# Two transformer layers on one core: a second static order of 3098 steps, with other engine homes and other PSUM banks

## The chip, the cores and the metric

The kernel runs on one core of one Trainium2 chip. A core has a matrix engine (TensorE, PE in the profile, with its weight loads shown as PEld), a vector engine (VectorE, DVE), an activation engine (ScalarE, ACT), a general engine (GpSimd, POOL), a queue that issues transfers (SyncE, SP) and 16 DMA engines. Each engine works through its own list of instructions in order; engines meet only at semaphores. The metric is the device time of one execution in microseconds, as a median over runs; less is better.

## What is computed

The input `x` is 2048 rows of 512 numbers in bf16. Four blocks follow one another, A, B, A, B, with the same weights each time:

```python
def _A_ref(x, wqkv, wo):
    H = 32; Dh = D // H; W = 256
    q, k, v = ...                       # x @ wqkv, split into 32 heads of 16
    scores = jnp.einsum("bhqd,bhkd->bhqk", q, k) * (Dh ** -0.5)
    mask = (i - j >= 0) & (i - j < W)   # a sliding window of 256 keys
    p = _softmax(jnp.where(mask, scores, -1e9))
    return jnp.einsum("bhqk,bhkd->bhqd", p, v) ... @ wo

def _B_ref(x, w1, b1, w2, b2):
    return _gelu(x @ w1 + b1) @ w2 + b2     # 512 -> 1792 -> 512

x = x + _A_ref(_layernorm(x), A_wqkv, A_wo)
x = x + _B_ref(_layernorm(x), B_w1, B_b1, B_w2, B_b2)
x = x + _A_ref(_layernorm(x), A_wqkv, A_wo)
x = x + _B_ref(_layernorm(x), B_w1, B_b1, B_w2, B_b2)
```

## The kernel before

All weights and the whole of `x` stay in SBUF. The work of both layers is cut into 16 attention blocks of 256 rows (8 per layer; b0 to b15) and ten MLP jobs of 256 or 512 rows (m0 to m9). Because the window is 256 keys, block b of the second layer needs only a few blocks of the first, so attention of one part runs beside the MLP of another.

One attention block consists of these steps, each with a short name that the texts below use with the block's number:

- layer norm: statistics `bs`, `ba` on VectorE; for all but the first pair of rows the inverse root on GpSimd (`vp` adds epsilon, on GpSimd or VectorE; `pw` is the power -0.5, on GpSimd); `xn` applies it on VectorE; a DMA transpose on SyncE's queue (`tx`) or, for the first four and the last two row tiles, a transpose on TensorE (`tp`) with an eviction `te` on VectorE or ScalarE
- projections `q`, `k`, `v` on TensorE, evictions `qe` and `ve` on VectorE or ScalarE, `ke` on VectorE; `vs` is a shifted copy of V by DMA
- 10 visits (5 in the first block of a layer): scores `sc` (TensorE, into four PSUM banks, allocated as two pairs), two exponentials `ex` on ScalarE that each free one pair, and masks `mk`, multiplications in place on VectorE or GpSimd
- twice per block `pv` (TensorE, probabilities times V, into a pair of banks), its transpose `od` out of PSUM, `rc`, `nm` (VectorE or GpSimd) and `ot`; `od` frees the pair of banks for the next scores
- the output projection `op` and the residual `rs`, and the second layer norm

An MLP job has 14 groups of first matmuls with gelu on ScalarE (six go through VectorE's `gb` and a paired gelu `ga`, eight are direct, `ge`), then per row tile 14 second matmuls `y` and the sum `ya` on VectorE with `Xb`, which GpSimd prepares (`xb`). The last row tile, y31, is done in two halves of 256 columns.

At the start 18 matmuls on zeros (`warm`) keep TensorE busy; GpSimd writes constants (among them `ia`, a memset of V's column of ones in all ten V buffers, `Va[:, :, :, Dh:VW]`, and `pidx`), and VectorE makes `parmask` from `pidx` in two small steps, `i5` and `i6`, which the first `ke` needs.

What sets the order is not the code's loops. Every step is recorded in a list of 3098 nodes (`add` in `_Plan`), and three tables replay it: `_ORDER` is the global sequence, from which each engine's list is the subsequence of its own steps (so it sets SyncE's transfers too); `_ALT` lists the steps that take their second home (a mask on GpSimd, an eviction on ScalarE, and so on); `_BANKS` gives the PSUM bank of each allocation in turn. `_Sched` then derives the semaphore waits from what each step reads and writes.

## Time and profile before

| | |
|---|---|
| median of 3 runs | 441.85 us (441.66 to 443.46) |
| span of the profiled execution | 442.4 us (its only time on the page; 0.55 us over the median, inside the runs' range) |
| TensorE busy | 416.1 us, 94% of the span |
| ScalarE busy | 386.4 us, 87% |
| VectorE busy | 341.0 us, 77% |
| GpSimd busy | 212.7 us, 48% |
| mean granted TensorE clock | 0.996 |

A window row reads: the stretch in us from the span's start, its length, then for each engine the busy us and the number of instructions, then the granted clock of TensorE (1.00 is full), the share of the DMA engines and GB/s. A timeline row reads: start, length, engine, line, operation, what it writes from what it reads, the shapes, the count of merged instructions, and in brackets how long the engine sat idle before and what released it. A row of the chain of waits reads: start, length, engine and line, count.

### The profile page before, as it was taken

The numbers are of one execution on the slowest core, as the hardware profiler recorded it, in microseconds if no ns is written. First come the engines' busy times: TensorE is split into PE (matmuls) and PEld (weight loads), VectorE is DVE, ScalarE is ACT, GpSimd is POOL, SyncE is SP. The second block draws the span as 40 slices with busy tenths as digits, with TensorE's granted clock in tenths as the row PEclk, the third lists the DMA queues.
The fourth block names the chain that finished last, engine by engine and source line by source line (L and its number), as shares of the span: only waits on it lengthen the run. The fifth ranks groups of instructions, "written<-read, shape, count | busy, mean of one in ns | idle before, by whom it ended". The sixth has DMA issues, their size and how long they took to land.

```text
span 442.4 us, 16864 instructions
## 1 busy us (share of the span) xinstructions
PE 416.1 (94%) x7523; PEld 233.2 (53%) x7593; DVE 341.0 (77%) x638; ACT 386.4 (87%) x458; POOL 212.7 (48%) x236
## 2 busy tenths in 40 slices
PE   8997999988789997999999999999999999999997
PEld 4555657544444563554455455455555464444675
DVE  7997789788785599967698868877888576746762
ACT  4997999999889999889899989999897988999533
POOL 3566344363442674711575454634728165804411
PEclk9999999999899999999999999999999999999999
DMA  7686422004101012121031021100421014003002
GB/s 234 184 209 185 87 64 45 20 10 69 39 3 25 16 34 56 28 46 24 4 65 31 1 57 26 34 20 10 69 39 20 20 39 105 14 1 81 15 0 73
DMA packets 48116, 23.25 MB, mean 53 GB/s; under 512 B 33196, under 2 KB 48044, under 8 KB 48044
## 3 DMA queue, kind: packets, MB, share of 16 engines
q1 hardware_dynamic: 48044, 22.17, 22.2%
q8 instruction: 60, 0.98, 0.9%
q14 instruction: 12, 0.10, 0.1%
HBM read 8.00 MB, written 2.10 MB: 23 GB/s over the span
## 4 chain that ended last, share of the span: by engine, by line
PE 79%; ACT 11%; DVE 6%; issue 2%; DMA 1%; DVEq 0%
PE ps L653 59%; PE ps L754 9%; PE ps L804 9%; ACT E L761 9%; DVE OD L813 1%; PE ps L539 1%; DVE stat L599 1%; DVE X L849 1%; DMA xnTB<-xn 1%; ACT gT L879 1%; ACT L879 1%; DVE KT L687 1%; DVE E L782 0%; PE ps L639 0%; ACT QT L590 0%
## 5 line engine op out<-in xcount | busy, mean ns | idle before, releaser
L761 ACT ACTIVATE E<-ps 128x1024 bf16<-128x1024 f32 x300 | 284.2, 1033 | 28.7 <-PE ps L754 28.0
L782 POOL TENSOR_TENSOR E<-E,mask 128x512 bf16<-128x512 bf16 (+2 forms) x111 | 120.9, 1106 | 91.3 <-ACT E L761 91.0
L653 PE MATMUL ps<-W_sb,gT 128*128 128x512 bf16 (+1 forms) x434 | 112.2, 373 | 3.2 <-issue 2.2
L653 PE MATMUL ps<-xnTB,W_sb 128*128 128x512 bf16 (+1 forms) x541 | 107.8, 336 | 3.4 <-issue 1.8
L653 PEld LDWEIGHTS ps<-xnTB,W_sb 128*128 128x128 bf16 x560 | 52.0, 98 | 42.9 <-issue 4.1
L653 PE MATMUL ps<-xnTA,Wqkv_sb 128*128 128x256 bf16 x512 | 70.7, 273 | 0.9 <-ACT E L761 0.4
L782 DVE TENSOR_TENSOR E<-E,mask 128x512 bf16<-128x512 bf16 (+2 forms) x125 | 60.1, 500 | 13.3 <-ACT E L761 12.9
L754 PE MATMUL ps<-QT,KT 32*128 32x128 bf16 (+3 forms) x1920 | 60.3, 231 | 9.8 <-ACT E L761 5.6
L653 PEld LDWEIGHTS ps<-W_sb,gT 128*128 128x128 bf16 x462 | 41.2, 98 | 41.1 <-issue 3.6
L754 PEld LDWEIGHTS ps<-QT,KT 32*128 32x128 bf16 x1920 | 28.5, 92 | 59.1 <-ACT E L761 34.9
L653 PEld LDWEIGHTS ps<-xnTA,Wqkv_sb 128*128 128x128 bf16 x512 | 47.4, 98 | 20.2 <-issue 2.9
L813 DVE STREAM_TRANSPOSE OD<-ps 128x1024 f32<-128x1024 f32 x32 | 39.9, 1246 | 21.3 <-PE ps L804 20.7
L887 POOL TENSOR_TENSOR Xb<-X,b2all 128x512 f32<-128x512 bf16 x32 | 37.7, 1180 | 34.3 <-DVE X L894 33.9
L879 ACT ACTIVATE gT<-ps,b1T 128x512 bf16<-128x512 f32 (+1 forms) x80 | 42.6, 609 | 9.5 <-PE ps L653 9.4
L804 PE MATMUL ps<-E,Va 64*17 64x128 bf16 (+3 forms) x1920 | 44.3, 234 | 1.9 <-issue 0.8
L821 POOL TENSOR_TENSOR Nb<-OD,Rc 128x512 bf16<-128x512 f32 x25 | 26.4, 1058 | 38.7 <-DVE Rc L817 29.8
L804 PE MATMUL ps<-E,Vs 64*17 64x128 bf16 (+3 forms) x1920 | 44.9, 234 | 0.0
L599 DVE BATCH_NORM_STATS2 stat<-X 128x6 f32<-128x512 bf16 x64 | 42.9, 679 | 0.5
L804 PEld LDWEIGHTS ps<-E,Va 64*17 64x17 bf16 x1920 | 37.2, 85 | 11.6 <-issue 9.0
L871 DVE TENSOR_SCALAR gT<-ps,b1T 128x512 bf16<-128x512 f32 (+1 forms) x60 | 36.8, 632 | 6.6 <-PE ps L653 6.2
L687 DVE TENSOR_TENSOR KT<-ps,parmask 128x1024 bf16<-128x1024 f32 x32 | 38.7, 1211 | 3.6 <-PE ps L653 3.6
L804 PEld LDWEIGHTS ps<-E,Vs 64*17 64x17 bf16 x1920 | 38.0, 85 | 0.2
(55 smaller groups left out, 348.8 us busy)
## 6 DMA issues: line engine op xcount, KB each, us to landing
Vs<-Va SPq DMA_DIRECT2D x64, 68.0 KB, 2.0
W_sb<-in_B_w_dram SPq DMA_DIRECT2D x4, 512.0 KB, 4.8
out_dram<-X SPq DMA_DIRECT2D x15, 128.0 KB, 1.8
X<-in_A_x_dram SPq DMA_DIRECT2D x3, 512.0 KB
Wqkv_sb<-in_A_wqkv_dram SPq DMA_DIRECT2D x4, 256.0 KB, 4.5
W_sb<-in_B_w_dram SPq DMA_DIRECT2D x2, 384.0 KB, 7.1
W_sb<-in_B_w_dram SPq DMA_DIRECT2D x1, 768.0 KB, 5.0
Wqkv_sb<-in_A_wqkv_dram SPq DMA_DIRECT2D x1, 512.0 KB, 6.7
```

Source lines behind the costliest of these rows:

```text
L599: add("dve", lambda e, B, t=t, k6=k6: e.bn_stats(stat6[:, k6, :], X[:, t, :]), reads=["X%d" % t], writes=["st%d" % k6], key="bs%d" % (k + j))
L653: r = e.matmul(ps[:, B[g][0], cols], lhsT, rhs, start=st, stop=sp)
L687: add("dve", lambda e, B, g=g, i=i: e.tensor_tensor(out=KT[:, kb, 2 * i : 2 * i + 2].rearrange("p c m a q -> p a (c m) q"), in0=ps[:, B[g] ...
L754: x = e.matmul(ps[:, bk[r], o : o + n], KT[rows, kb, c, m].rearrange("p a q -> p (a q)"), QT[rows, c, q : q + n], start=True, stop=True)
L761: add("act", lambda e, B, g_=g_, gi=gi: e.activation(E[:, 2 * gi : 2 * gi + 2, e0 : e0 + 512], ps[:, B[g_][0] : B[g_][0] + 2, :], AF.Exp, ...
L782: fn = lambda e, B: e.tensor_tensor(out=Ew, in0=Ew, in1=Mw, op=ALU.mult)
L804: x = e.matmul(ps[32 * r : 32 * r + VW, B[g][par], c % 2 * 2 * P + lo : c % 2 * 2 * P + hi], V[rows, (2 * b + m // 2) % VR, c * HC + 2 * r ...
L813: add("dve", lambda e, B: e.transpose(OD[:, s].rearrange("p a c q -> p (a c q)"), ps[:, B[g][0] : B[g][0] + 2, :]), reads=["ps:" + g], wri ...
L821: return e.tensor_tensor(out=Nb[:, s, :].rearrange("p (k a d) -> p a k d", a=2, d=Dh), in0=sums[:, :, :, 0:Dh], in1=rc[:, :, :, None].to_b ...
L871: add("dve", lambda e, B, g=g, fc=fc: e.tensor_scalar(out=gT[:, fc, c0 : c0 + M], in0=ps[:, B[g][0], 0:M], scalar1=b1T[:, fc : fc + 1], sc ...
L879: add("act", lambda e, B, g=g, fc=fc: e.activation(gT[:, fc, c0 : c0 + M], ps[:, B[g][0], 0:M], AF.Gelu_apprx_tanh, bias=b1T[:, fc : fc + ...
L887: add("pool", lambda e, B, t=t, xs=xs: e.tensor_tensor(out=Xb[:, xs, :], in0=X[:, t, :], in1=b2all[:], op=ALU.add), reads=["X%d" % t, "b2a ...
```

## The change

The three tables are replaced; nothing else is. The computation, the instructions' shapes and the number of steps are the same. Of the engine homes, the following differ (counted from the two programs): ScalarE holds 1 instead of 3 of the `te`, 14 instead of 13 of the `qe` and 8 instead of 10 of the `ve`; GpSimd holds 103 instead of 111 of the 236 masks, 24 instead of 25 of the `nm` and 18 instead of 21 of the `vp`. VectorE takes the rest, 653 steps instead of 638. 43 masks move from GpSimd to VectorE and 35 the other way. The number of times ScalarE alternates between exponential and gelu work is the same, and in the same pattern. Line numbers of all code behind the tables fall by 7.

```diff
 _ORDER = [
-    15, 34, 5, 0, 6, 14, 35, 7, 33, 28, 38, 29, 47, 8, 18, 23, 9, 36, 3, 26, 31, 10, 57, 37, 11, 22, 1, 40, 4, 24,
...
+    35, 15, 5, 0, 34, 8, 32, 31, 38, 9, 17, 47, 10, 27, 28, 1, 37, 23, 2, 3, 59, 22, 36, 19, 40, 60, 4, 57, 16, 63,
...
 ]
 
 _ALT = [
-    67, 70, 75, 102, 109, 116, 121, 148, 165, 170, 185, 192, 198, 202, 211, 216, 337, 342, 370, 374, 378, 384, 389,
...
+    70, 75, 102, 109, 121, 148, 165, 170, 192, 198, 202, 211, 216, 337, 342, 374, 378, 383, 384, 389, 393, 406, 411,
...
 ]
 
 _BANKS = [
-    0, 1, 0, 1, 0, 2, 3, 2, 3, 5, 7, 0, 6, 5, 3, 2, 5, 4, 2, 4, 2, 3, 3, 5, 0, 1, 2, 6, 1, 5, 2, 4, 6, 1, 0, 2, 4, 6,
...
+    4, 3, 1, 0, 2, 5, 6, 3, 2, 4, 3, 5, 2, 4, 2, 6, 3, 4, 7, 3, 5, 0, 6, 1, 3, 2, 6, 5, 1, 3, 4, 6, 1, 0, 2, 4, 7, 6,
...
 ]
```

The first place is the start of the program. VectorE's list before, from the statistics of row tiles 2 and 3 to the keys of blocks 0 and 1 (`BN_STATS` is bs, `BN_AGGR` ba, L611 vp2, L574 the cast of the bias, L627 the xn of tiles 3 and 2, L687 ke, L588 COPY a te):

```order
L599 BN_STATS stat<-X 128x6 x2
L601 BN_AGGR statmv<-stat 128x2 x2
L611 TENSOR_SCALAR rstd<-statmv 128x2
L574 CAST b1T<-ps 128x14
L627 TENSOR_SCALAR xn<-X,statmv,rstd 128x512 x2
L687 TENSOR_TENSOR KT<-ps,parmask 128x2x8x64
L588 COPY xnTA<-ps 128x4x128
L599 BN_STATS stat<-X 128x6 x2
L601 BN_AGGR statmv<-stat 128x2 x2
L687 TENSOR_TENSOR KT<-ps,parmask 128x2x8x64 x2
```

and VectorE's list in the changed program from the eviction of row tile 0 on (one BN_STATS of the pair stands just ahead of it):

```order
L581 COPY xnTA<-ps 128x4x128
L594 BN_AGGR statmv<-stat 128x2
L592 BN_STATS stat<-X 128x6
L514 TENSOR_SCALAR pidx<-pidx 128x2
L594 BN_AGGR statmv<-stat 128x2
L567 CAST b1T<-ps 128x14
L604 TENSOR_SCALAR rstd<-statmv 128x2
L620 TENSOR_SCALAR xn<-X,statmv,rstd 128x512
L516 TENSOR_SCALAR parmask<-pidx 128x2
L620 TENSOR_SCALAR xn<-X,statmv,rstd 128x512
L680 TENSOR_TENSOR KT<-ps,parmask 128x2x8x64
L581 COPY xnTA<-ps 128x4x128 x2
```

The two small steps on pidx, which stood ahead of all statistics, now stand among them; the evictions of row tiles 0 and 3 have come over from ScalarE; the bias cast has moved ahead of vp2. GpSimd's list at the same place, before:

```order
L511 MEMSET ident 128x128
L536 MEMSET Va 128x320
L525 MEMSET mask 128x192
L528 AFFINE_SELECT mask<-mask 128x64
L518 MEMSET mhalf 128x2
L528 AFFINE_SELECT mask<-mask 128x64 x2
L512 AFFINE_SELECT ident<-ident 128x128
L515 AFFINE_SELECT ident<-ident 128x128
L617 TENSOR_TENSOR rstd<-rstd,mhalf 128x2
```

and in the changed program:

```order
L504 MEMSET ident 128x128
L518 MEMSET mask 128x192
L521 AFFINE_SELECT mask<-mask 128x64 x2
L505 AFFINE_SELECT ident<-ident 128x128
L508 AFFINE_SELECT ident<-ident 128x128
L511 MEMSET mhalf 128x2
L610 TENSOR_TENSOR rstd<-rstd,mhalf 128x2
L529 MEMSET Va 128x320
L521 AFFINE_SELECT mask<-mask 128x64
```

The memset of Va has moved from the second place to the place right behind the power step that releases the first xn of VectorE's list above.

The second place is ScalarE's list in blocks 3 to 6, from the switch to the exponential table behind job m1 to the switch behind it. Before:

```order
L761 ACT_TABLE_LOAD
L761 ACTIVATE E<-ps 128x2x512 x21
L590 ACTIVATE QT<-ps 128x2x256
L761 ACTIVATE E<-ps 128x2x512
L590 ACTIVATE QT<-ps 128x2x256
L761 ACTIVATE E<-ps 128x2x512 x11
L590 ACTIVATE QT<-ps 128x2x256
L761 ACTIVATE E<-ps 128x2x512 x13
```

and in the changed program:

```order
L754 ACT_TABLE_LOAD
L754 ACTIVATE E<-ps 128x2x512 x22
L583 ACTIVATE QT<-ps 128x2x256
L754 ACTIVATE E<-ps 128x2x512 x11
L583 ACTIVATE QT<-ps 128x2x256
L754 ACTIVATE E<-ps 128x2x512 x13
```

One of three query evictions (qe6_1) has left ScalarE for VectorE; the 46 exponentials stay in this list (two neighbours in block 4 change places).

The third place is the end of TensorE's list. Before:

```order
L653 MATMUL ps<-xnTB,W_sb 128x256 x2
L653 MATMUL ps<-W_sb,gT 128x256
L653 MATMUL ps<-xnTB,W_sb 128x256 x2
L653 MATMUL ps<-W_sb,gT 128x256 x23
L653 MATMUL ps<-W_sb,gT 128x512 x14
```

and in the changed program:

```order
L646 MATMUL ps<-W_sb,gT 128x256
L646 MATMUL ps<-W_sb,gT 128x512 x3
L646 MATMUL ps<-W_sb,gT 128x256
L646 MATMUL ps<-W_sb,gT 128x512 x4
L646 MATMUL ps<-W_sb,gT 128x256 x13
```

Row tile 30 in full width (14 matmuls of 512 columns) came last; now a half of row tile 31 (256 columns) does.

## Prediction

> **What bounds the kernel now.** I read the shares first, then the stretches in time, then who waits for whom, and last the starts of the three engines' own timelines.

> ```profile
> PE 416.1 (94%) x7523; PEld 233.2 (53%) x7593; DVE 341.0 (77%) x638; ACT 386.4 (87%) x458; POOL 212.7 (48%) x236
> ```

> TensorE is busy 416.1 of 442.4 us, so 26 us is all that a new order can win. The stretches say where those lie:

> ```profile
> 20.00:45.00 25.00, 21.51 (x497) 13.69 (x488) 21.37 (x40) 22.50 (x27) 15.23 (x19) 1.00 0.73 185
> 45.00:95.00 50.00, 48.15 (x863) 30.06 (x877) 43.04 (x87) 47.90 (x63) 21.90 (x24) 1.00 0.23 47
> 95.00:130.00 35.00, 28.52 (x794) 16.76 (x776) 28.04 (x50) 31.33 (x35) 15.13 (x18) 0.95 0.21 36
> 130.00:195.00 65.00, 60.77 (x1198) 32.64 (x1207) 51.82 (x103) 59.35 (x66) 37.18 (x39) 1.00 0.17 33
> 195.00:440.00 245.00, 238.94 (x4043) 129.29 (x4083) 179.07 (x325) 211.24 (x250) 114.15 (x119) 1.00 0.15 33
> 0.00:10.00 10.00, 8.49 (x55) 4.98 (x56) 7.58 (x21) 5.30 (x9) 4.03 (x15) 1.00 0.75 220
> 10.00:20.00 10.00, 9.70 (x119) 5.77 (x118) 9.97 (x18) 8.82 (x12) 5.09 (x7) 1.00 0.79 226
> ```

> Three regimes follow. From 10 to 20 us VectorE has no slack (9.97 of 10). From 20 to about 130 us ScalarE is the full engine (47.90 of 50 in the second row), and TensorE idles 6.5 us in 95 to 130. From 195 us on TensorE is busy 238.94 of 245 (97.5%) and what another engine does there is mostly covered. The waits and the chain agree:

> ```profile
> PEld ps L754 <- ACT E L761: 34.9, 80, 1.5
> ACT E L761 <- PE ps L754: 28.0, 50, 1.8
> 22.33 3.77 ACT E L761 x4
> 107.70 8.46 ACT E L761 x9
> ```

> The scores' weight loads wait for exponentials to free banks, and exponentials wait for scores; the chain runs through ScalarE in long pieces in the early part.

> **The start: VectorE's queue gets longer (term 1).**

> ```profile
> 1.10 1.46 POOL L536 MEMSET Va<- 128x320 bf16 x1
> 1.36 1.38 DVE L521 TENSOR_SCALAR pidx<-pidx 128x2 int32<-128x2 int32 x1
> 2.77 0.17 DVE L523 TENSOR_SCALAR parmask<-pidx 128x2 f32<-128x2 int32 x1
> 7.29 0.17 DVE L611 TENSOR_SCALAR rstd<-statmv 128x2 f32<-128x2 f32 x1
> 7.37 0.17 DVE L574 CAST b1T<-ps 128x14 f32<-128x14 bf16 x1
> 7.54 0.71 POOL L617 TENSOR_TENSOR rstd<-rstd,mhalf 128x2 f32<-128x2 f32 x1 [3.29 <-DVE b1T L574]
> 8.29 0.73 DVE L627 TENSOR_SCALAR xn<-X,statmv,rstd 128x512 bf16<-128x512 bf16 x2 [0.76 <-POOL rstd L617]
> 9.40 1.22 DVE L687 TENSOR_TENSOR KT<-ps,parmask 128x1024 bf16<-128x1024 f32 x1 [0.38 <-PE ps L653]
> 10.69 0.40 PE ps L754 x8
> 22.12 1.25 DVE L813 STREAM_TRANSPOSE OD<-ps 128x1024 f32<-128x1024 f32 x1 [0.37 <-PE ps L804]
> L588 DVE COPY xnTA<-ps 128x512 bf16<-128x512 bf16 x1 | 0.4, 414 | 0.0
> ```

> Before, epsilon (L611) is added at 7.29, the power follows on GpSimd, the two xn at 8.29, the first keys at 9.40, and the first scores at 10.69, right behind them. The change puts ahead of L611 an eviction COPY (0.41), the pidx step (0.17, as its twin on the row at 2.77 took without company) and the bias cast (0.17): 0.75 us. The parmask step stands between the two xn: 0.17. Of these 0.92 the keys had 0.38 to spare, waiting for TensorE: the first keys and scores come 0.55 us later.

> From the keys to the first OD (9.40 to 22.12) VectorE runs without a gap worth naming, and the change adds the eviction of tile 3 (0.41) and two masks ahead of that OD:

> ```profile
> L782 DVE TENSOR_TENSOR E<-E,mask 128x768 bf16<-128x768 bf16 x47 | 26.0, 571 | 8.3 <-ACT E L761 8.2
> L782 DVE TENSOR_TENSOR E<-E,mask 128x512 bf16<-128x512 bf16 x59 | 29.6, 513 | 4.7 <-ACT E L761 4.6
> ```

> One of 768 columns comes forward from behind it (0.57), one of 512 comes from GpSimd (0.51). That is 1.49, less the 0.37 for which OD waited: 1.1. OD frees two banks for block 1's second scores; ScalarE hides some 0.3 of it, since its exponentials there stand one behind the other. Term 1: 0.55 + 1.1 - 0.3 = +1.35, between 0.2 (if the queue's slack elsewhere takes it) and 1.65. The two evictions taken off ScalarE there buy nothing: it waits at that time.

> **A collision in the start (term 2).** GpSimd's memset of Va took 1.46 us, and beside it the pidx step took 1.38 instead of 0.17. The memset now stands right behind the power step, which is what releases xn. Has an xn been seen stretched beside GpSimd? The view of its line says so:

> ```profile
> L627 DVE TENSOR_SCALAR xn<-X,statmv,rstd x64: 315/408/1266, 4.7 to 424.1; 128x512 bf16<-128x512 bf16 x64
> ```

> median 408 ns, longest 1266. So one of the two xn, with the keys behind it in the queue, waits for the memset: between 0 and 1.4 us; I take +1.2, nearest to the pidx row (1.38 - 0.17). [...]

> **Transfers and the first MLP job.** SyncE's list moves two loads (the last rows of x, the last piece of W1) from the start to behind the first transposes to xnTB, and puts other weight pieces ahead of V's shifted copies. In 20 to 45 us the DMA engines are busy 0.73, so a transpose may land sooner or a weight later by about 1 us; ScalarE covers both there, and I take 0, with 0.8 either way. The xn of tile 9 stands ahead of block 1's first OD (0.41); half of it reaches the scores behind: +0.2, from 0 to 0.4.

> **The stretch bound by ScalarE (term 3).**

> ```profile
> L590 ACT ACTIVATE QT<-ps 128x512 bf16<-128x512 f32 x13 | 8.0, 613 | 1.6 <-PE ps L653 1.6
> L590 ACT ACTIVATE Va<-ps 128x512 bf16<-128x512 f32 x10 | 6.1, 625 | 1.1 <-PE ps L653 1.0
> ```

> Between 45 and 130 us ve8 and qe6_1 leave ScalarE and qe4_0 comes to it: -0.63 - 0.61 + 0.61 = -0.63. VectorE is busy 28.04 of 35 there and takes them. A full engine's saving goes through: -0.63, from -1.25 (both removals, the addition covered) to 0 (VectorE's masks late in turn, with `pv` behind them).

> **The later part.** Masks and nm change homes; over the whole program VectorE gains 15 steps and GpSimd loses 12. From 195 us TensorE has 6 us of idle time in 245, scattered; I take 0, within 1 us either way.

> **The end (term 4).**

> ```profile
> 439.39 0.69 DVE L894 TENSOR_TENSOR X<-Xb,ps 128x512 bf16<-128x512 f32 x1 [2.20 <-PE ps L653]
> 436.44 0.75 DVE L894 TENSOR_TENSOR X<-Xb,ps 128x256 bf16<-128x256 f32 x2 [4.23 <-PE ps L653]
> out_dram<-X SPq DMA_DIRECT2D x15, 128.0 KB, 1.8
> out_dram<-X SPq DMA_DIRECT2D x2, 64.0 KB, 1.7
> ```

> The last sum is now a half (0.75 for two overlapped, so about 0.42) in place of 0.69, and its store 1.7 in place of 1.8: -0.35, from -0.4 to 0.

> **Sum.** +1.35 + 1.2 + 0.2 - 0.63 - 0.35 = +1.8 us. The profiled execution spans 442.4, so 444.2; the median stands 0.55 below that span, so 443.6.

> **Rivals.**

> *No collision.* [...] For it: most xn keep to 408 ns. Against: the pidx row. The sum without term 2 is +0.6: 442.4.

> *Faster: relief on ScalarE goes through and the clock stays up.*

> ```profile
> 38.00:41.40 3.40, 2.02 (x29) 1.22 (x27) 2.48 (x3) 3.05 (x4) 1.03 (x1) 1.00 0.40 77
> 113.10:116.50 3.40, 1.69 (x32) 1.02 (x28) 3.05 (x7) 3.40 (x5) 0.23 (x1) 1.00 0.20 41
> 116.50:119.90 3.40, 2.89 (x138) 2.16 (x132) 0.71 (x1) 3.00 (x4) 1.22 (x2) 0.50 0.20 41
> 116.79 2.32 PE ps L804 x125
> 149.29 1.37 PE ps L804 x119
> ```

> Behind 3.4 us with only 1.69 of matmul work the granted clock is 0.50 for 3.4 us, and a `pv` in it takes 2.32 instead of 1.37; behind 2.02 it stays at 1.00. If the fuller packing of the changed order keeps that stretch above such a level, 0.95 us returns; with term 3 at -1.25, term 1 at its low end of 0.2, no collision and the end at -0.35, the sum is -2.35, and -2.85 if the later part gives half of its 1: 439.0. Against it: the exponentials of block 4 stand almost as before, so TensorE has as little to do there.

> *Slower: the clock is halved in the start as well.* With terms 1 and 2, TensorE has between its first key matmuls and those of block 1 hardly more than one set of scores (0.40) and two transposes, for some 3 us: less than the 1.69 that was followed by half clock. For 3.4 us its work then takes twice as long, up to 1.7 us, while ScalarE waits for it: 443.6 + 1.7 = 445.3. It decides once that pause passes about 2 us inside one such window. Against it: where the window lies is chance. [...]

> *Slower: a mask that came to VectorE holds up `pv` in 95 to 130.* VectorE is busy 80% there and every `pv` waits for its last mask, every score behind for that `pv`'s banks. Three such delays of about 0.8 us (a mask behind a residual and a statistic of 0.69 each, partly hidden) give +2.4: 446.0. Against: 35 masks leave it too.

> **How the numbers follow.** A difference under 0.5% (2.2 us) is about what these runs cannot tell from none. Forecast 0.36 (443.6, its own range 442.6 to 444.7), no collision 0.20 (442.4), faster 0.15 (439.0), half clock 0.18 (445.3), late masks 0.11 (446.0). Under 439.6: most of the faster case, 0.14. Over 444.1: both slow cases and a third of the forecast's upper part, 0.40. Between: 0.46. The range 439.4 to 446.4 leaves out about half of the faster case and of the late masks' tail.

> **What would show it.** Term 1: the first scores near 11.2 us (12.4 with the collision) instead of 10.69, and the first OD over 1 us later than 22.12. Term 2: an xn of about 1.6 us, or a Va memset lengthened, near 9 us. Term 3: ScalarE busy as before in 45 to 130 but ending the 46 exponentials 0.6 us nearer to their start. Term 4: the last VectorE row of 256 columns. I am wrong if the first scores come no later, if the second half holds more idle time than 6 us, or if the clock rows differ.

## The result and the profile after

| | before | after |
|---|---|---|
| median | 442.19 us (441.66 to 443.46, 4 runs) | 460.42 us (459.53 to 461.07, 4 runs) |
| span of the profiled execution | 442.4 us | 457.6 us |
| mean granted TensorE clock of it | 0.996 | 0.985 |
| number of half-clock windows of 3.4 us | 1 | 4 |

The changed kernel takes 1.0405 times as long, 95% interval 1.038 to 1.043. The forecast was 443.6 us in a range of 439.4 to 446.4, so the time lies 14 us above the range. Here and below, ratios and intervals leave out the slow executions, those more than 1.5% above the fastest of their kernel; medians and ranges hold all of them.

The shares of the engines, from the page of after:

```profile
PE 431.7 (94%) x7593; PEld 233.4 (51%) x7593; DVE 347.6 (76%) x653; ACT 385.5 (84%) x455; POOL 203.2 (44%) x224
```

TensorE's share is 94% as before, which says nothing. The trace of before lacks 70 of 7,593 matmul records. Run b4 below, the same program without two short warm-up products and at the same time, has all of its records and shows TensorE busy 424.2 us where the trace of before shows 416.1, so about half of the rise to 431.7 is missing records; matmuls at half clock, which are longer, are part of the rest (a projection matmul of 256 columns took a mean of 414 ns from 35.9 to 39.3 us, at half clock, and 284 from 39.3 to 59.7, at full). It also shows that the prediction read too much idle time into TensorE. From 45 to 95 us its row is:

```profile
45.00:95.00 50.00, 49.04 (x906) 30.00 (x904) 42.70 (x86) 47.88 (x63) 21.93 (x24) 1.00 0.25 46
```

TensorE is at least as full there as ScalarE, so what holds it up there is not covered. The stretches of after, in the same columns as those of before:

```profile
20.00:45.00 25.00, 21.82 (x453) 12.97 (x452) 22.57 (x40) 19.26 (x24) 12.31 (x14) 0.93 0.58 153
45.00:95.00 50.00, 46.76 (x810) 29.44 (x806) 34.65 (x70) 42.23 (x58) 22.87 (x23) 0.93 0.37 73
95.00:130.00 35.00, 28.44 (x686) 15.26 (x684) 30.73 (x58) 32.43 (x36) 17.35 (x20) 1.00 0.32 51
195.00:440.00 245.00, 241.97 (x4212) 125.03 (x4211) 188.55 (x347) 218.80 (x251) 110.87 (x113) 1.00 0.16 31
```

From 195 us on TensorE is busy 241.97 of 245. In 45 to 95 us it did 810 matmuls where the trace of before shows 863 and that of b4 906, and ScalarE, which had been busy 47.90 of 50, only 42.23. The loss is ahead of 140 us for the most part. Where it arises is seen by setting the same steps of the two traces beside each other (the start of a step's first matmul in us, worked out from the two traces by the order of the steps; `scB_V` is visit V of block B, and `end` is the end of VectorE's last sum):

```
step      before   after   later by
sc0_0      10.7     12.1     1.4
sc1_3      28.6     29.9     1.3
sc1_5      33.9     39.7     5.8
pv1_1      49.7     52.7     3.0
sc2_1      55.7     65.4     9.6
sc4_2     107.2    117.1     9.8
sc5_1     126.5    138.9    12.4
sc13_0    325.4    338.3    12.9
sc14_1    362.3    377.1    14.7
end       440.1    455.5    15.4
```

There are four steps down: the start (1.3), 28 to 40 us (4.5, of which 2.8 comes back by 50 us), 53 to 65 us (6.6) and 117 to 139 us (2.6), and one more of 1.8 near 375 us. The chain of waits of after, from 27 to 61 us, shows the second and third:

```profile
27.68 4.39 DMA xnTA<-xn
32.17 0.41 DVE xn L620
32.58 1.07 DVE Nb L814
33.66 1.16 DVE E L775
34.82 0.63 DVE OT L820
35.50 4.24 PE ps L646 x18
...
57.55 3.03 issue
60.59 1.44 PE ps L646 x5
```

The transpose of row tile 6, `tx6`, landed 4.39 us after 27.68. xn8 (row tile 8) writes the buffer that this transpose reads, and the change has put it on VectorE ahead of nm and ot of block 0 and a mask of block 1, so all of these came late and with them op0. The 18 matmuls behind it took 4.24 us, at half clock. At 57.55 us TensorE stood still for 3.03 us with nothing that the profile shows to wait for. The fourth step is again a transpose, the one for the first matmuls of job m2:

```profile
124.32 1.20 SPq L625
126.26 4.55 DMA xnTB<-xn
130.85 1.33 PE ps L646 x4
```

and the last is a second pause of the kind of 57.55 us, in the middle of a `pv`:

```profile
374.93 1.65 issue
376.58 0.54 PE ps L797 x39
```

The clock rows, each 3.4 us long: the three windows in which TensorE had little to do, and the four at half clock that follow them.

```profile
32.50:35.90 3.40, 1.48 (x7) 0.52 (x7) 3.40 (x5) 2.13 (x3) 3.40 (x3) 1.00 0.95 292
35.90:39.30 3.40, 3.40 (x15) 2.09 (x14) 2.36 (x5) 0.00 (x0) 0.41 (x1) 0.50 0.46 146
56.40:59.80 3.40, 1.15 (x6) 0.40 (x5) 1.08 (x2) 1.31 (x4) 1.27 (x2) 1.00 1.01 259
59.80:63.20 3.40, 2.62 (x10) 1.38 (x10) 0.00 (x0) 0.76 (x2) 0.00 (x0) 0.50 0.43 41
63.20:66.60 3.40, 3.40 (x22) 1.72 (x21) 2.14 (x3) 2.04 (x3) 0.00 (x0) 0.50 0.19 39
128.10:131.50 3.40, 0.71 (x10) 0.31 (x4) 2.15 (x3) 1.00 (x2) 1.07 (x2) 0.99 0.70 29
131.50:134.90 3.40, 3.40 (x20) 1.03 (x18) 1.35 (x2) 1.94 (x2) 0.10 (x1) 0.50 0.00 0
```

An estimate from the granted 0.50: four such windows cost up to half their length each, 6.8 us; before there was one, 1.7 us. So up to 5 of the 15 us are half clock behind pauses, and the pauses are what has to be explained.

### What the unexplained pauses are

The page's list of queues has an entry that the prediction did not read, the same before and after:

```profile
q8 instruction: 60, 0.98, 0.9%
```

Sixty packets of 16 KB on a queue of their own; TensorE's list has 15,353 records in the trace of after, weight loads, matmuls and semaphore steps together, 255.9 to a packet. The pauses of 57.55, 115.6 (1.48 us) and 374.93 us stand ahead of TensorE's instructions 1,730, 3,778 and 12,994, counted in the trace by start: they are 2,048 and 9,216 apart, which is 8 and 36 times 256. (The one at 115.6 us is only in part such a pause: the scores behind it also wait for an exponential that ends at 116.10 us, and the profile puts the whole wait down to ScalarE.) And at the first of them the queues read so, from 52.8 to 58.0 us and then from 58.0 to 60.6 us (packets, MB, time as a share of the 16 engines):

```profile
q1 hardware_dynamic: 1586, 1.16, 123.8%
...
q8 instruction: 1, 0.02, 2.7%
```

In the first stretch the transfers filled the DMA engines and no instruction packet was started; it began at 58.13 us by its record, 5.2 us after TensorE had entered the block of 256 ahead of it, landed at 59.26, and TensorE went on at 60.59. For 49 of the 59 packets that have a block ahead the record begins no later than 1.5 us after the block ahead was entered. The theory from this (F below): TensorE's own instructions arrive in blocks of 256, one block ahead, and where a block is run through faster than the next one arrives, TensorE pauses.

### The profile page after: what moved, and what is told of

Read it like the earlier page. It is cut to its first block, busy times and chain, and to the rows that moved or that the text cites. A ratio compares the mean times of both kernels' runs of the same rounds, so it can differ in the third digit from the quotient of the medians.

```text
span 457.6 us, 16937 instructions
## 1 busy us (share of the span) xinstructions
PE 431.7 (94%) x7593; PEld 233.4 (51%) x7593; DVE 347.6 (76%) x653; ACT 385.5 (84%) x455; POOL 203.2 (44%) x224
## 4 chain that ended last, share of the span: by engine, by line
PE 74%; ACT 8%; DVE 8%; DMA 4%; issue 3%; SPq 1%; POOL 0%; DVEq 0%
PE ps L646 58%; PE ps L747 9%; PE ps L797 8%; ACT E L754 7%; DMA xnTB<-xn 3%; DVE stat L592 2%; DVE E L775 1%; DVE xn L620 1%; DMA xnTA<-xn 1%; SPq L625 1%; DVE KT L680 1%; ACT gT L872 1%; DVE X L842 1%; DVE X L887 1%; DVE OD L806 1%
## 5 line engine op out<-in xcount | busy, mean ns | idle before, releaser
L754 ACT ACTIVATE E<-ps 128x1024 bf16<-128x1024 f32 x300 | 283.5, 1037 | 41.5 <-PE ps L747 40.5
L775 POOL TENSOR_TENSOR E<-E,mask 128x512 bf16<-128x512 bf16 (+2 forms) x103 | 112.7, 1106 | 121.9 <-ACT E L754 121.5
L646 PE MATMUL ps<-xnTB,W_sb 128*128 128x512 bf16 (+1 forms) x560 | 116.4, 341 | 4.2 <-DMA xnTB<-xn 3.4
L646 PE MATMUL ps<-W_sb,gT 128*128 128x512 bf16 (+1 forms) x462 | 117.4, 375 | 3.0 <-issue 3.0
L646 PE MATMUL ps<-xnTA,Wqkv_sb 128*128 128x256 bf16 x512 | 74.7, 280 | 1.1 <-DMA Wqkv_sb<-in_A_wqkv_dram 0.4
L775 DVE TENSOR_TENSOR E<-E,mask 128x768 bf16<-128x768 bf16 (+2 forms) x133 | 62.5, 492 | 5.1 <-ACT E L754 4.8
L747 PEld LDWEIGHTS ps<-QT,KT 32*128 32x128 bf16 x1920 | 28.6, 93 | 58.3 <-ACT E L754 34.9
L646 PE MATMUL ps<-Wo_sb,OT 128*128 128x512 bf16 x128 | 39.6, 389 | 1.9 <-DVE OT L820 1.0
## 6 DMA issues: line engine op xcount, KB each, us to landing
out_dram<-X SPq DMA_DIRECT2D x15, 128.0 KB, 1.9
```

Source lines behind the costliest of these rows:

```text
L646: r = e.matmul(ps[:, B[g][0], cols], lhsT, rhs, start=st, stop=sp)
L747: x = e.matmul(ps[:, bk[r], o : o + n], KT[rows, kb, c, m].rearrange("p a q -> p (a q)"), QT[rows, c, q : q + n], start=True, stop=True)
L754: add("act", lambda e, B, g_=g_, gi=gi: e.activation(E[:, 2 * gi : 2 * gi + 2, e0 : e0 + 512], ps[:, B[g_][0] : B[g_][0] + 2, :], AF.Exp, ...
L775: fn = lambda e, B: e.tensor_tensor(out=Ew, in0=Ew, in1=Mw, op=ALU.mult)
```

## The experiments

The theories were S, that SyncE's list makes the loss (transposes, V copies and weights in an order that delivers late); F, that part of the pauses is TensorE's instruction blocks; and as rivals Q and R, that the lists of the compute engines make it, or that the lists as a whole lack slack, so that one wait gives way to the next. In the lists below `ldx`, `ldw`, `ldu`, `ldz` and `ldb` are loads of x, Wqkv, W1, W2 and the biases, `ldwo` that of Wo, `tx` transposes by row tile (from 32 on for the MLP), `vs` V copies. Line numbers are those of each kernel's own text and differ by a few.

### SyncE's list put back, as a whole and in parts

```diff
 SyncE's list, a1_sync_of_before
-ldx1 ldx0 ldx2 ... tx5 ldu0 vs3_0 vs2_1 vs2_0 tx7 tx6 ldwo vs3_1 ldz1 ldu1 ldz2 tx33 ...
+ldx0 ldx1 ldx2 ... tx5 vs2_1 ldu2 ldwo tx6 vs2_0 ldb2 tx7 vs3_1 vs3_0 ldu0 ldu1 ...
```

> The changed kernel with SyncE's list in the order of the kernel before; PE's, VectorE's, ScalarE's and GpSimd's lists, homes and banks stay the changed ones. Theory S (SyncE's list made the loss: transposes late behind V copies and weights near 28 to 35 us and at 126 to 131 us, the late loads of 46 to 58 us): the 3.03 us pause ahead of y1.6 near 57.5 us is gone, op0 no longer waits for Wo, the transpose for m2 lands earlier, and the time falls from 460.4 to 446 us (442 to 450). Rival Q (the lists and homes of the compute engines made it, SyncE only follows them): at most 4 us come back, 456 us or more. Both leave the late start (+1.4 us at the first scores).

Measured: 460.19 us (459.04 to 462.27), ratio to before 1.0418, 95% interval 1.0389 to 1.0448. By the time alone this is rival Q. The trace says something else: sc1_5, sc2_1 and sc5_1, 5.8, 9.6 and 12.4 us late in the changed kernel, are 2.3, 2.3 and 3.0 us late, the 3.03 us pause is gone, and there is no half clock before 384 us. Most of what came back was lost again from 310 us on, above all here (TensorE's timeline):

```profile
383.84 0.28 PE L797 MATMUL ps<-E,Va 64*17 64x256 bf16 x4 [4.00 <-DMA Vs<-Va]
```

SyncE's old order waits there for an xn that the changed VectorE forms late (its transpose is issued at 373.07 us), and nine more entries, of 0.6 to 1.7 us each, stand between it and the V copy that this `pv` needs. So the whole list was the wrong size of edit: right for the first part, in conflict with the others later.

```diff
 SyncE's list, b1_sync_of_before_early
 first 76 entries as in a1 above; from there on
-the order of before
+the changed order
```

> The changed kernel with SyncE's first 76 entries (up to about 140 us) in the order of the kernel before, and the rest of its list in the changed order; all other lists, homes and banks stay the changed ones. In the run with the whole list of before, the first scores of block 5 came 9.4 us earlier than in the changed kernel, and a 4.0 us wait for a V copy near 380 us and what follows gave it back. Theory S: the early part of that gain stays and the late wait doesn't come, 450 us (447 to 453). Rival (what is gained early is lost later whatever SyncE does, because another engine's list sets the end): 456 us or more.

Measured: 455.08 us (451.98 to 456.14), ratio 1.0275 (1.0229 to 1.0321), between the two expectations. In the profiled execution, the fastest of the four and at full clock, sc5_1 is 3.4 us late and VectorE's last sum 7.8.

```diff
 SyncE's list, a2_loads_early
-... ldw2_0 ldw0_256 ldx8 vs1_1 ... ldu1 ldz2 tx33 tx32 tx9 ldu2 vs6_1 ldb2 ldz0 vs6_0 ldz3 tx8 ldx12 vs7_0 ...
+... ldw2_0 ldx12 ldw0_256 ldx8 ldz2 vs1_1 ... vs2_0 ldu2 tx7 tx6 ldb2 ldwo vs3_1 ldz1 ldu1 ldz3 ldz0 tx33 ...
```

> The changed kernel with only the six late loads (X from row 12 on, the second and third W1 piece's ldu2, b2, W2's pieces 0, 2 and 3) put back to about the places in SyncE's list that they had before; all else stays. Theory F (the pause ahead of y1.6 is TensorE waiting for its own instructions: a block of 16 KB on the instruction queue that lands at 59.26 us because the transfers of 50 to 58 us fill the DMA engines): the instruction packet of that place starts within 2 us of the block ahead being entered in place of 5.3 us, the 3.03 us pause and the two half-clock windows behind it go, 453 us (451 to 456). Rival (a semaphore or data that y1.6 waits for, whatever the loads): the pause stays, 459 to 461 us.

Measured: 455.11 us (449.35 to 459.36), ratio 1.0227 (1.0158 to 1.0296). The pause at y1.6 is gone. That step stands at 58.8 us now, and the stretch around it reads:

```profile
53.00:61.00 8.00, 8.00 (x177) 5.57 (x175) 4.66 (x9) 7.54 (x15) 3.05 (x4) 1.00 0.11 23
```

TensorE is busy 8.00 of 8.00 at full clock, with the DMA engines at 0.11, and the packet of that place began 1.0 us after the block ahead was entered in place of 5.2. This is what theory F expects. It isn't decisive, since the edit also brings three pieces of W2 earlier, which the `y` steps read; run a4 below decides. The gain is 5.3 us between the medians, 8 us by the ratios.

```diff
 SyncE's list, a3_transposes_first
-... tx5 ldu0 vs3_0 vs2_1 vs2_0 tx7 tx6 ldwo vs3_1 ... vs12_1 tx39 vs11_0 tx38 ...
+... tx5 tx7 tx6 ldwo ldu0 vs3_0 vs2_1 vs2_0 vs3_1 ... tx39 tx38 vs12_1 vs11_0 ...
```

> The changed kernel with only these moves in SyncE's list: the transposes of blocks 7 and 6 and the load of Wo ahead of W1's first piece and the V copies of blocks 3 and 2 (near 21 us), and the transposes of xn39 and xn38 ahead of the V copy of block 12 (near 123 us). Theory S: xn8 no longer waits 1.1 us for its buffer, op0 finds OT and Wo there, the half clock of 35.9 to 39.3 us goes, -3 to -4.5 us; m2_3 waits 1.4 us less of 2.7 us and may keep the full clock, -1 to -3 us; 455 us (453 to 458). Rival Q (VectorE's order, xn8 ahead of nm0_1 and the mask, is what counts at 31 to 40 us): 458 to 461 us.

Measured: 451.61 us (448.75 to 455.03), ratio 1.0222 (1.0159 to 1.0285): 8.8 us back, more than expected, though a block pause of 2.36 us still stands ahead of y1.6. The four runs fall in two pairs by their granted clock: 449.65 and 448.75 us at 1.000, 455.03 and 453.57 us at 0.996. One window at half clock more, with the pause that brings it on, goes with 5 us.

### More of the places mended at once

```diff
 b2_and_start_of_before: b1, and the lists and homes of VectorE, ScalarE and GpSimd in the first 12 us
-VectorE ib bs1 ba1 ie bs0 rr1 ba0 xn1 rr0 xn0 bs3 te0 ba3 bs2 i5 ...   GpSimd i4 i0 i7 ... pw2 ia j10 ...
+VectorE ib i5 i6 bs0 ie ba0 bs1 rr0 ba1 xn0 rr1 xn1 bs3 bs2 ba2 ...    GpSimd i4 i0 ia i7 ... pw2 ...
```

> The run with SyncE's first 76 entries, and VectorE's, ScalarE's and GpSimd's lists of the first 12 us in the order and with the homes of the kernel before as well (the memset of Va early, i5 and i6 early, the first transposes' evictions te0 and te3 on ScalarE). Theory T (the late start of 1.4 us, the prediction's first two terms, is carried through to the end): the first scores at 10.7 to 11.0 us in place of 12.1, and the time 1 to 1.5 us under the run without it. Rival (the stretch bound by ScalarE or the later waits absorb it): within 0.5 us of the run without it.

Measured: 451.52 us (448.31 to 454.92), ratio 1.0207 (1.0137 to 1.0277). The first scores stand at 11.3 us in place of 12.4 in b1, later than the 10.7 to 11.0 expected. The time is 3.6 us lower, but the two ranges overlap, so the size of the start's part isn't told by the times.

```diff
 c2_places_mended: the moves of a2 and a3, the start of b2, and in VectorE's list
-... od0_1 rc0_1 xn8 nm0_1 mk1_2_1 ot0_1 ...
+... od0_1 rc0_1 nm0_1 mk1_2_1 ot0_1 xn8 ...
```

> The changed kernel with only the places that the trace named put right: in SyncE's list the six loads back early, the transposes of blocks 7 and 6 and the load of Wo ahead of W1's first piece, xn39's and xn38's transposes ahead of the V copy of block 12; the lists and homes of the first 12 us as before; and xn8 behind ot0_1 in VectorE's list. All else, TensorE's order and the banks too, as changed. Theory S (the loss stands at these places): the gains of the runs with the parts, 5.3 and 8.8 us, lie at different places for the most part, and 1.4 us for the start, so 446 us (443.5 to 449.5). Rival (the lists lack slack as a whole, and one wait gives way to the next): 451 us or more.

Measured: 451.41 us (449.00 to 456.66), ratio 1.0167 (1.0128 to 1.0206): no more than a3 alone, the rival's case. Its chain of waits has a new piece:

```profile
28.38 5.91 DMA Wo_sb<-in_A_wo_dram
```

Wo stood behind two transposes whose xn were late, was not issued until 28.38 us and landed 5.91 us later, and op0 waited for it. So that was mended too:

```diff
 e1_places_and_wo_first: SyncE's list
-ldx1 ldx0 ... tx5 tx7 tx6 ldwo ldu0 ...
+ldx0 ldx1 ... tx5 ldwo tx7 tx6 ldu0 ...
```

> The run with the places mended, and two things more in SyncE's list: the load of Wo right behind the transpose of block 5, ahead of those of 7 and 6 (in that run it stood behind them, whose xn was late, was issued at 28.4 us and landed at 34.3 us, and TensorE waited 1.75 us for it at op0), and the first 13 entries, the first rows and weights, as before. VectorE's, ScalarE's, GpSimd's and TensorE's lists as there. Theory S (the loss stands at named places, and the rest of that run's +7.7 us at the end is half Wo): the step sc1_7 comes 3 to 4 us earlier than there, and the time is 446 us (443.5 to 449). Rival (one wait gives way to the next and the half clock comes with any pause): 449.5 us or more.

Measured: 453.64 us (448.50 to 455.59, 6 runs), ratio 1.0209 (1.0169 to 1.0249). The rival again. sc1_5 came 4.0 us earlier than in c2, sc1_7 only 2.4, and then the chain reads:

```profile
33.28 4.23 DMA Vs<-Va
37.51 0.35 issue
37.87 1.43 PE ps L797 x116
...
42.20 2.54 issue
```

Now a V copy was late, and behind it a TensorE instruction block, its packet 3.8 us behind the entry into the block ahead, with the transfers again at 1.06 of the DMA engines. The named places are worth 5 to 9 us of the 18 by the medians. Beyond that, mending one brings up the next.

### The changed lists put into the kernel before

```diff
 SyncE's list, c1_before_with_changed_sync (all other tables as before)
-ldx0 ldx1 ... tx5 vs2_1 ldu2 ldwo tx6 vs2_0 ldb2 tx7 vs3_1 ...
+ldx1 ldx0 ... tx5 ldu0 vs3_0 vs2_1 vs2_0 tx7 tx6 ldwo vs3_1 ...
```

> The kernel before with SyncE's first 76 entries (up to about 125 us) in the changed order (two loads, ldu2 and ldb2, stand 2 to 4 places earlier than there, which the lists of before require), the rest of its list, all other lists, homes and banks as before. Theory S (SyncE's order alone brings the loss of the first 130 us): the 9.4 us that putting it back gave come as a loss, 450 us (446 to 455), with a pause ahead of y1.6 in which TensorE's instructions land late. Rival P (SyncE's order costs only together with the changed lists of VectorE and TensorE, which took the slack): 445 us or less.

Measured: 459.61 us (458.62 to 462.17), ratio 1.0392 (1.0355 to 1.0428). SyncE's early list alone is enough to lose as much as the whole change, and more than was expected. The waits that it makes:

```profile
PE ps L646 <- DMA W_sb<-in_B_w_dram: 4.9, 1, 4.9
POOL Xb L880 <- DMA b2all<-in_B_b_dram: 3.8, 1, 3.8
PE ps L646 <- DMA xnTB<-xn: 2.0, 1, 2.0
PE ps L646 <- DMA Wo_sb<-in_A_wo_dram: 1.2, 1, 1.2
```

The 4.9 us stand at y1.0, near the changed kernel's 3.03 us pause, but here a piece of W2 was late, not the instructions as expected; b2 held GpSimd and through it VectorE. c1 also has six windows at half clock, which cost up to 10 us. The changed kernel's own list of waits has none for W2 or b2. They come about because SyncE stands for 10.8 us, until 56.4, at the transpose of row tile 9, whose xn VectorE's old list forms late (at 50.54 in the kernel before, at 42.32 in the changed one). So c1 shows what an entry that waits in SyncE's list can cost, and not the share of that list in the changed kernel's 18 us. The two halves of this list apart:

```diff
 SyncE's list, d3_before_loads_late: only six loads moved
-... ldw2_0 ldx12 ldw0_256 ldx8 ldz2 ... vs2_1 ldu2 ldwo tx6 vs2_0 ldb2 ... ldu1 ldz3 vs5_1 tx32 tx33 ldz0 ...
+... ldw2_0 ldw0_256 ldx8 ... vs2_1 ldwo tx6 vs2_0 ... ldu1 ldz2 vs5_1 ldu2 ldb2 tx32 tx33 ldz1 vs4_0 tx8 ldz0 ldz3 ldx12 ...

 SyncE's list, d4_before_rest_changed: the list of c1 with those six about where they stood
+... ldw2_0 ldx12 ldw0_256 ldx8 ldz2 ... tx5 ldu0 vs3_0 vs2_1 ldu2 vs2_0 ldb2 tx7 tx6 ldwo vs3_1 ...
```

> The kernel before with only six loads late in SyncE's list, about where the changed kernel has them: X from row 12 on, ldu2, ldb2 and W2's pieces 0, 2 and 3 (ldb2 and ldu2 a little earlier than there). Theory L (the late loads are the larger part of SyncE's loss: b2 late holds Xb and through it VectorE, a W2 piece that lands at 62.9 us holds TensorE for 4.9 us near 58 us): 452 us (447 to 457). Rival T (the order of transposes, V copies and Wo is the larger part): 443 to 446 us.

> The kernel before with SyncE's first 76 entries in the changed order except those six loads, which stand where they stood: what is changed are the transposes, the V copies, Wo, W1's first piece and the first rows and weights. Theory L: 446 us (443.5 to 449), from op0's wait for Wo (2 us) and the transposes for the second MLP jobs near 126 us. Rival T: 452 us or more.

Measured: 450.81 us (450.09 to 452.32), ratio 1.0194 (1.0170 to 1.0218), and 453.98 us (452.33 to 454.81), ratio 1.0257 (1.0231 to 1.0283). 8.5 and 11.7 us: neither is the larger part by far, and their sum, 20, is close to the 17 of both. The first is as theory L expected, and in its trace GpSimd waits 6.1 us for b2, which the changed kernel doesn't. The second is what rival T expected, above theory L's 446; there SyncE waits 10.0 us for an xn. So both hold losses that come from the order that the other lists of before are made for, which the next pair shows in full:

```diff
 d1_before_with_changed_compute
-VectorE's, ScalarE's, GpSimd's lists and homes of before
+the changed ones; TensorE, SyncE and banks stay
 d2_before_with_changed_tensor
-TensorE's list and banks of before
+the changed ones; all other lists and homes stay
```

> The kernel before with VectorE's, ScalarE's and GpSimd's lists and homes as changed (a few entries stand up to 7 places from there, which TensorE's list of before requires), and with TensorE's list, banks and SyncE's list as before. These are the lists on which the prediction's terms 1 to 4 rest (start, memset beside xn, ScalarE's work, tail). Theory P (those terms are right and the rest of the loss is SyncE's): 443.6 us (441.5 to 446). Rival R (the changed compute lists lack slack at more places than the four terms, as the 455 us with SyncE's early list put back suggests): 449 us or more.

> The kernel before with TensorE's list and the banks as changed, all other lists and homes as before (a few entries up to 11 places from there). Theory N (TensorE's list is only perturbed locally; it costs the one pause of 1.65 us where the instruction block of 375 us lands late): 443.5 us (441.5 to 446). Rival R (the changed place of the steps in TensorE's list makes it wait for results that come in the old order): 449 us or more.

Measured: 567.55 us (563.52 to 571.61) and 570.74 us (567.91 to 573.48). Theories P and N are off by over 120 us, and rival R's "449 us or more" holds without having foreseen the size. From the page of the first:

```profile
PE 443.3 (79%) x7523; PEld 237.5 (42%) x7593; DVE 351.9 (63%) x653; ACT 390.7 (70%) x457; POOL 203.6 (36%) x224
```

The engines' work is hardly more than before: TensorE's busy time is at least 19 us above b4's 424.2, at a lower clock (0.943), VectorE's and ScalarE's 11 and 4 us above before, GpSimd's 9 below, and the span 119 us longer, so all stand idle for longer. The pauses lie all over the program, and the steps fall back steadily, to 25 us at sc6_0, 49 at sc11_0 and 97 at sc15_0. Yet among the entries that keep their engine VectorE's are displaced by only 2.9 places on average and ScalarE's by 0.8. Lists that were made for one another could not be exchanged one at a time here: this pair tells nothing of which list of the changed kernel is worse, and c1, d3 and d4 hold some of the same.

### The instruction blocks

```diff
 a4_blocks_shifted (changed kernel) and b3_before_blocks_shifted (kernel before)
-e.matmul(ps[:, B[g][0], 0:n], gT[:, 0, 0:P], gT[:, 0, 0:n], start=True, stop=True)
+for c in range(k):   # k = 4 for the eleven of 512 columns
+    r = e.matmul(ps[:, B[g][0], c*n//k:(c+1)*n//k], gT[:, 0, 0:P], gT[:, 0, c*n//k:(c+1)*n//k], start=True, stop=True)
```

> The changed kernel with its eleven warm-up products of 512 columns issued as four of 128 columns each, so that TensorE's program is 33 weight loads and 33 matmuls longer from the start, with the same columns; everything behind is unchanged. Theory F (blocks of 256 TensorE instructions are fetched, and the pauses near 57.5 and 374.9 us stand at the first instruction of a block that landed late): each pause moves 33 matmuls earlier in the program: the first into the step pv1_1 (an attention product of 128 matmuls), 14 matmuls before its end, where no semaphore can hold it, at about 55.5 us, and it ends again near 60.5 us, so it grows from 3.0 to 4 to 6 us; time 458 to 464 us. Rival (y1.6 waits for data or a semaphore): the pause stays ahead of y1.6, 3.0 us long, and the time within 1 us of 460.4.

Measured: 468.81 us (465.36 to 470.06), ratio 1.0595 (1.0553 to 1.0638), above the range of both. The pause has left y1.6 and stands inside pv1_1, 12 matmuls before its end, ahead of the 849th matmul of the trace as it was ahead of the 848th, and of instruction 1,730 as there:

```profile
57.71 0.26 PE L802 MATMUL ps<-E,Vs 64*17 64x192 bf16 x4 [2.19 <-issue]
```

This program puts a step's semaphore waits ahead of its first instruction, and none stands in the middle of one, so the place is F's; the length, 2.19 us, is less than the 4 to 6 expected. What was not expected is the 8.4 us of loss: the shift gave new pauses at other blocks, of 0.7 to 2.3 us.

> The kernel before with its eleven warm-up products of 512 columns issued as four of 128 columns, 66 instructions more on TensorE from the start, nothing else changed. Theory F (each block of 256 TensorE instructions is fetched while the block ahead runs, which takes some 3.5 us, and where the block ahead runs faster than that TensorE pauses; an attention product step alone is 256 instructions in 1.4 to 2 us): the time of each 256 instructions in the trace of before, taken 66 instructions earlier, gives pauses of 12 us in sum at about ten places, 452 us (448 to 457). Rival (the shift cost 8 us in the changed kernel because of that kernel's own crowded transfers): 441.5 to 444 us.

Measured: 459.23 us (457.78 to 459.96), ratio 1.0376 (1.0347 to 1.0405): 17 us from 33 pairs of weight load and matmul at the start, about what the whole change lost and above the 448 to 457 expected. The pauses in its chain of waits:

```profile
36.52 2.87 issue
...
152.68 1.31 issue
...
182.12 2.67 issue
...
198.64 2.09 issue
...
246.32 1.94 issue
```

They sum to 10.9 us, and each stands a multiple of 256 away from those of the changed kernel in TensorE's list. The half clock behind them (mean 0.988, so 1.2% of the span) adds up to 5.5 us. Since the kernel before has pauses of this kind too (next run), some 2 us of the 17 are not accounted for.

```diff
 b4_before_two_less: the emission loop of the kernel before
+if nd["key"] in ("warm9", "warm10"):
+    continue
```

> The kernel before without two of its warm-up products of 32 columns (they compute nothing that is used), four TensorE instructions less from the start. Theory F: the boundaries of the blocks stand 4 instructions later in the program; of the two pauses of 1.23 us at 39 and 106 us the sum of short blocks in the trace falls from 1.4 to 0.9 us: 441.3 us (440 to 442.2). Rival (the boundaries are nothing that the time hangs on): 441.8 to 442.4 us.

Measured: 442.51 us (442.25 to 442.77, 10 runs), ratio 1.0002 (0.9991 to 1.0012). The two pauses of 1.23 us are gone from the trace and the time is the same, about as the rival had it. ScalarE ran exponentials through both (38.35 to 40.29 and 105.53 to 107.47 us in the trace of before), and the first 0.5 us or so of each is TensorE's wait for the first of these. So a block pause behind ScalarE costs nothing here; that it costs where TensorE itself is the bound, or where it brings the half clock, is how a4 and b3 read.

## Why the prediction was wrong

**The step that failed is "Transfers and the first MLP job".** It saw that SyncE's list moves loads and puts weights ahead of V copies, counted the DMA engines as busy 0.73, and put the whole at 0, with 0.8 us either way. Put back in part, that list gives 5.3 us (the loads, a2), 8.8 (transposes and Wo, a3) or 5.3 (its first 76 entries, b1); put into the kernel before, it costs 17, in part by waits that the changed kernel doesn't have. What was overlooked is that SyncE works in order too: a transpose waits there for an xn, and all weights and V copies wait behind it (at 16 waits for an xn SyncE stood 153.9 us in sum in the trace of after). The two transposes that were late took 4.39 and 4.55 us to land, where the median of their kinds in this trace is 2.5 and 2.7. "ScalarE covers both there" fails because op0, y1 and m2 are not behind exponentials: in the three windows ahead of the half clock ScalarE is busy 2.13, 1.31 and 1.00 us of 3.40. The premise behind it, that ScalarE alone is full from 20 to 130 us, was read from a trace with missing matmul records.

**Half clock (a rival for the start, 0.18).** That it follows a window with little matmul work was right, the place and the number were not: the granted clock stayed at 1.00 in the first 30 us, and four windows came later, behind three pauses. Behind 1.48, 1.15 and 0.71 us of matmul work in 3.4 us the granted clock was 0.50. That agrees with the 1.69 us before. The longest pause in the first of these windows is 0.97 us.

**Terms 1 and 2, the start (+2.55 forecast): measured +1.3.** The collision is there, as these rows of VectorE's and GpSimd's timelines show:

```profile
8.53 1.46 POOL L529 MEMSET Va<- 128x320 bf16 x1
8.62 1.52 DVE L620 TENSOR_SCALAR xn<-X,statmv,rstd 128x512 bf16<-128x512 bf16 x1 [0.83 <-POOL rstd L610]
10.16 0.40 DVE L620 TENSOR_SCALAR xn<-X,statmv,rstd 128x512 bf16<-128x512 bf16 x1
12.08 0.12 PEld L747 LDWEIGHTS ps<-QT,KT 32*128 32x128 bf16 x8 [0.91 <-DVE xnTA L581]
23.40 1.22 DVE L806 STREAM_TRANSPOSE OD<-ps 128x1024 f32<-128x1024 f32 x1
```

One xn took 1.52 us beside the memset and the other 0.40, a price of 1.12 where 1.2 was taken, and the first scores came at 12.08 us where 12.4 was forecast with the collision. What did not come is the 1.1 us between the keys and the first OD: from the keys (9.40 before, 10.48 after) to the OD (22.12 and 23.40) it was 12.72 and 12.92 us. VectorE had idled 0.6 us in it, where the prediction saw no gap but the 0.37 ahead of OD, and now not at all; its busy time there rose by 0.8, from 12.11 to 12.90, and not by 1.5.

**Term 3 (-0.63) can't be seen.** From sc2_1 to sc4_2, where ScalarE's queue was to be shorter, the lateness stays at 9.6 to 9.8 us.

**The later part (0, within 1): measured +3.0** from sc5_1 to the end. 1.8 of it comes with the block pause of 1.65 us at 375 us. This pause came back in a2, a3, b1 and b2 with 1.65 to 1.92 us, its packet beginning 4.8 to 5.1 us after the block ahead was entered, though in the changed kernel's trace the DMA engines had nothing to do for the first 3 us of that. Why it begins so late there, no run tells.

**Term 4 (-0.35): about -0.5.** The last sum is a half now, 0.42 us; the end of the span lies 15.2 us later, that of the last matmul 15.7.

**What stays open.** Of the 18 us, 5 to 9 are shown to be SyncE's order. The start is 1.3 us in the trace, the block pauses of the changed kernel are at most 6.2 us against 2.5 before (three of these five hold a wait for an exponential as well), and half clock up to 5 us more, but these overlap with the first and with one another, and some pauses lie where ScalarE covers them. So the cause of about half of the loss stays open. Whether VectorE's or TensorE's new list would be slower with a SyncE list made for it, the experiments can't say, since lists of different origin lose over 100 us when mixed.

None of the mended kernels beats the kernel before.

## What to carry to other kernels

Treat the queue that issues transfers as an engine with an order of its own: for every entry that moves, ask what it now waits behind and what waits behind it, and don't let a share of DMA time under 1 (0.73 here) stand for "hidden". Treat static lists of several engines as one object: here a part of one could be mended, and the lists of the compute engines or of TensorE, exchanged as a whole, cost over 100 us. Where a program has thousands of short TensorE instructions, look at the instruction queue as well, and keep in mind that what is added at the start can move the time of everything behind: here 66 instructions more cost 8.4 us in the changed kernel (a4) and 17 in the kernel before (b3), and four fewer nothing (b4).
